# New due times for a delta-rule and two-FFN program, and set fetches queued ahead of the store in front of them

## The chip, the cores and the metric

The program runs on one core of one Trainium2 chip. The metric is the device time of one execution in microseconds (us); for the kernel before, three runs were taken, and one more execution was recorded by the hardware profiler. The engines are TensorE (PE; its weight loads are PEld), VectorE (DVE), ScalarE (ACT), GpSimd (POOL) and SyncE (SP), which here issues most of the DMAs.

## What is computed

The reference runs three parts one after another, in float32. First a delta-rule recurrence over 768 positions for 4 x 8 heads of width 40, then a squared-ReLU FFN (320 to 2048 to 320) on 3072 tokens, then a second FFN that mixes four domains by given probabilities:

```python
for t in range(S):
    y[:, :, t] = np.einsum('bhd,bhde->bhe', rt, state)
    Sa = np.einsum('bhde,bhe->bhd', state, at)
    state_decay = state * wt[:, :, None, :] - np.einsum('bhd,bhe->bhde', Sa, bt)
    state = state_decay + np.einsum('bhd,bhe->bhde', vt, kt)
...
h = x @ w_in
r = np.maximum(h, 0.0)
g = r * r
return (g @ w_out).astype(np.float32)
...
p = domain_probs / (domain_probs.sum(-1, keepdims=True) + 1e-09)
for e in range(E):
    h = np.maximum(x @ w1[e], 0.0)
    out += p[:, e:e + 1] * (h @ w2[e])
```

## The kernel before

**First half.** The 768 positions are cut into 12 chunks of 64 and two batch halves, which gives 24 "steps"; two steps (one chunk) make a "block", so there are 12 blocks. A step multiplies small matrices on PE: `m` (L545, L547), `vm` (L593, L597), `f` (L624), `kbt` (L610), `x` (L637), `merge1` (L679), `merge2` (L691), `tx` (L714), `ys` (L726) and `s` (L754), with copies on ACT and masks, scans and reciprocals on DVE (`vmm` L602, `txm` L718, `P` L488, `rq` and `rs` L508). The triangular inverse inside a chunk is done for a whole block at once on DVE: `m` leaves PE, is copied by ACT and stored to DRAM (`mo`, L563, tile md), loaded back turned (`tl`, L791, tile mu), worked on by 62 dependent DVE operations (`t`, L808 and L811), turned by ACT (`tt`, L818), stored (`to`, L823, tile td) and loaded into the two steps (`ti`, L832, eight DMAs into t and TT). Only then can `merge1` and `merge2` of the two steps run, and behind them `tx`, `x`, `ys` and the new state. A block's result is gathered by twelve DMAs (`tx1`, L919) and split into two float32r parts (`x1h` L930, `x1l` L933); the first FFN then runs 16 "units" on it, each of 8 matmuls `l1` (L317), squaring on ACT (L870 to L875), a difference `gl` on DVE (L878), and 6 matmuls `l2` (L322, L323, L326). In the first 150 us, 48 weight pieces are prepared as well (`w_ld` L345, DVE operations L371 to L378, PE `w_pe` L358 to L360).

**What sets the order.** All of these operations are given to `Schedule`, which replays them on a model of the engines while the program is built and so fixes the order in which each engine's instructions stand; on the chip each engine works through its own list in that order. At every turn the replay takes the engine that can start first and, among its operations that could start within `DELAY` of that, the one with the earliest due time. A due time is the block's or step's base, from `DUE`, less an entry of `LEAD`; an operation of PE in another array tiling than the last counts as due `STAY` later, and up to `COLD` the replay counts PE at half speed. The numbers in these tables are durations in no program: they only choose the order.

**Second half.** The second FFN has 6 pairs of token blocks and 4 weight "sets" for each of 4 domains, so 96 steps. A step is a Strassen-like product of 28 or 32 matmuls (`products` L1225 to L1228, or `plain` L1269 to L1272), whose sums DVE makes (L1233), and 24 matmuls `pz` (L1294 to L1296) of the step before. Its tiles stay in SBUF; 16 sets do not fit, so while a domain runs, the four sets of the next one are prepared one after another (`prepare`): SP loads the raw weights (`set_load`, L1065 and L1066 to L1067, tiles wm and wr), DVE sums them (`set_sum`), ACT rounds them (`set_round2` from wr and `set_round` from wm, L1019), DVE takes the low parts (L1022), and for three of the four SP stores the finished set to DRAM (`set_store`, L1104) because all four are built in the same spare tiles; POOL fetches them later (`set_fetch`, L1108). POOL also fetches each pair's X from DRAM (`x_fetch`, L1197). A class `Beside` deals these jobs out to the steps by a number `due`, by what they depend on, and by `lag`: so many steps must lie between a job and the one that it depends on, if that is on another engine. Before the change a set's load depended on the store of the set in front:

```python
l = job("sp", 0.9, set_load, n, deps=prev, after=after, due=D[0])
w = [job(rnd, 0.36, set_round2, s, i, deps=[l], lag=2, due=D[2], after=s.free) for i in range(2)]
...
if store:
    return [job("sp", 1.8, set_store, s, deps=lo, lag=0, due=D[4])]
return lo + [d]
```

Of the kernel before, what the change touches and what calls it, by code (L numbers as in the profile page):

```python
# [14 lines left out]
B, H, S, D = 4, 8, 768, 40  # L15
# [27 lines left out]
def sub(base, dims):  # L43
# [2 lines left out]

DUE = dict(block=63.76, step=[98.3, -158.9, 2.4, -355.2, -9], invert=[-219.9, -0.6, -157.6], ffn=0.2, w=[-205.6, 1.33])
LEAD = dict(  # L50
    ld_wd=894.9, ld_in=421.6, scan=77.5, m=303, t_load=135.5, t=345.2, t_out=384.9, ld_r=-259.7, ld_xv=-166,
    vm=93.4, f=84.3, kbt=47.4, x=66.9, merge=66.1, tx=131.2, ys=374.4, yq=75.2, x1=185.5,
    split=112.7,
)
DELAY = dict(PE=0.21, ACT=0, DVE=0, POOL=0, SP=0.53)


class Schedule:

    COLD = 54.3  # L60
    STAY = 20.28
    SAME = 0.033

    TILING = dict(vm=1, f=1, tx=1, x=2, ys=2, m=3, merge1=4, merge2=4)
# [10 lines left out]
        m=(.58, .65), vm=(.985, 1.12), kbt=(.41, .6), tx=(.775, .94), f=(.62, .67), merge1=(.62, .69), merge2=(.62, .69),  # L75
        s=(.44, .62), kb=(1.18, 1.25), yq=(.70, .74), scale_a=(1.22, 1.27), yf=(.41, .45), te=(.95, .9), yg=(.16, .2),
# [3 lines left out]
        ld_in=(.43, 2.85, 1.67), ld_r=(.42, .94, 1.45), ld_rf=(.45, .6, 1.65), ld_v=(.45, 1.0, 1.3), ld_wd=(.43, 1.08, 1.35),  # L80
        ld_xv=(1.28, .55, 1.9), mo=(.46, .33, .91), ti=(.46, .28, 1.35), tl=(.58, 1.44, 1.62), to=(.70, 1.05, 1.19),
# [3 lines left out]
        DVE=("P", "t", "x1l", "sq", "w_clamp", "w_shift", "w_sign", "w_pow", "w_mul"),  # L85
        POOL=("scale_a", "kb", "yq", "yf", "y1d", "yg"),
# [103 lines left out]
class Beside:  # L190
# [5 lines left out]
    def job(self, eng, dur, fn, *a, deps=(), lag=1, due=0, after=-99, key=None, via=None):  # L196
        self.n += 1
        key = key or self.n
        engs = (eng,) if isinstance(eng, str) else eng
        self.jobs[key] = (due, self.n, engs, dur, fn, a, deps, lag, after, via)  # L200
        return key
# [66 lines left out]
def tile_delta_rule_moe(  # L268
# [15 lines left out]
    pe, act, dve, pool, sp = nc.tensor, nc.scalar, nc.vector, nc.gpsimd, nc.sync  # L284
# [496 lines left out]
    mdd, x1 = {}, {}  # L781
# [190 lines left out]
    nblk = nsteps // 2  # L972
    PB, F0 = DUE["block"], 80.0
    units = NF1 * (nblk - 1)
    for s in range(nsteps):
        attention(s, F0 + PB / 2 * s + DUE["step"][min(s, len(DUE["step"]) - 1)])
    for k in range(nblk):
# [7 lines left out]
    ffn = []  # L985
# [329 lines left out]
    job = plan.job  # L1315
    NP = NF1 + 2

    done = {}
    for P in range(NPAIR):
        k, e = 2 * P, NPW * P  # L1320
        D = {0: (-50, -15, -13, -12, -10, -7, -8, -4, -2, 0, 1), 1: (-11, -9, -10, -8, -1, 1, 1, 3, 4, 5, 5)}.get(
            P, tuple(e + d for d in (-7, -5, -5, -4, -1, -3, -2, -1, 0, -1, 0)))
# [34 lines left out]
        job("sp", 0.45, x_store, P, 6, 7, deps=b6 + [("st", P, 0)], due=e + 5, key=("st", P, 6))  # L1357

    def prepare(s, D, after, rnd, store, prev, single=False):
        n = s.n  # L1360
        l = job("sp", 0.9, set_load, n, deps=prev, after=after, due=D[0])
        w = [job(rnd, 0.36, set_round2, s, i, deps=[l], lag=2, due=D[2], after=s.free) for i in range(2)]
        lo = [job("dve", 0.41, set_low2, s, i, deps=w[i:i + 1], due=D[4]) for i in range(2)]

        def part(x, y, deps, due, after, lag=1):
            r = [job(rnd, 0.05 + (y - x) / 960, set_round, s, c, x, y, deps=deps, due=due[0], after=after, lag=lag) for c in range(2)]
            q = job("dve", 0.07 + (y - x) / 960, set_rest, s, x, y, deps=r[1:], due=due[1])
            lows = [(max(x, a), min(y, b)) for a, b in ((0, 384), (384, 768), (768, 896)) if max(x, a) < min(y, b)]
            return r + [q] + [job("dve", 0.07 + (b - a) / 960, set_low, s, a, b, deps=r[:1], due=due[1]) for a, b in lows]

        d4 = D[2], D[4]
        if not single:
            m = [job('dve', 0.72, set_sum, n, *z, deps=[l], lag=2 if after >= 0 else 3, due=D[1]) for z in SUMS]
            lo += part(0, 384, m, d4, s.free) + part(384, 896, m, d4, s.free)
            d = job("sp", 0, set_done, s, deps=lo, lag=0, due=D[4], key=("set", n))
        else:
            lo += part(0, 512, [l], d4, s.free, lag=2)
            d = job("sp", 0, set_done, s, deps=lo, lag=0, due=D[4], key=("set", n))
        if store:
            return [job("sp", 1.8, set_store, s, deps=lo, lag=0, due=D[4])]  # L1380
        return lo + [d]

    homes, spare = list(range(NPW)), NPW
    prev = []
    for n in range(NPW):
        s = Set(n, homes[n], 3 * homes[n] + 4 - NP)
        D = ((-14, -18, -10, -9, -7), (-9, -10, -4, -2, -2), (-8, -5, 2, 2, 1), (-7, -1, 1, 1, 2))[n]
        prepare(s, D, -NP - 1, ("dve", "act"), False, [], True)
    for e in range(NE - 1):
        for i in range(NPW):  # L1390
            n = NPW * (e + 1) + NPW - 1 - i
            b = PER * e + (4 if e == 0 else 0) + 5 * i
            prev = prepare(Set(n, spare, b), tuple(b + d for d in ((0, 8, 8, 8, 8) if e else (-2, 0, 5, -7, 0))), b, ("act",), i < NPW - 1, prev)
# [3 lines left out]
    for G in range(NPAIR, NE * NPAIR):  # L1397
        e, i = divmod(G, NPAIR)
# [4 lines left out]
    i = -NP  # L1403
# [131 lines left out]
```

## Time and profile before

| | |
|---|---|
| median of 3 runs | 1474.74 us (1464.42 to 1477.5) |
| profiled execution | 1474.95 us |
| its span, first to last instruction | 1473.2 us |
| PE / DVE / ACT / POOL busy | 1381.4 / 1082.5 / 785.1 / 207.8 us |
| mean granted clock of PE | 0.971 |

The span falls into a start of some 216 us, in which the weights are prepared and the first blocks run, a steady part up to 752 us with one block after another, and the second FFN. "Granted clock" is the share of TensorE's full 2.4 GHz that was given; it has two levels here, 1.0 and 0.5 (1.2 GHz), so a mean between them tells how long the lower one held. In the chain of waits, "DMA x<-y" is a transfer from its issue to its landing, and SPq is SP issuing. In a timeline the bracket behind a row is the engine's idle time before it and what ended that.

### The profile page before, as it was taken

What the parts mean: (1) busy time and instruction counts of PE and PEld (TensorE: products, weight loads), DVE (VectorE), ACT (ScalarE), POOL (GpSimd) and SP (SyncE); (2) the same over time, 40 slices, a digit from 0 to 9 for tenths busy, and PEclk for the clock granted to TensorE, in tenths of its full rate; (3) what the DMA queues carried; (4) which work ended last, traced back from release to release, by engine and by line L of the source; (5) the groups of instructions that cost most, each with busy time, mean ns of one, the idle gap of its engine ahead of it and who ended that gap; (6) DMA issues with size and microseconds to landing.
All of it is one profiled execution on the core that took longest, in us unless ns stands there. A gap on an engine that the chain in (4) does not pass through costs nothing.

```text
span 1473.2 us, 39713 instructions
## 1 busy us (share of the span) xinstructions
PE 1381.4 (94%) x16072; PEld 1312.5 (89%) x16072; DVE 1082.5 (73%) x2664; ACT 785.1 (53%) x1933; POOL 207.8 (14%) x327
## 2 busy tenths in 40 slices
PE   4698999989999999999989999999999999999998
PEld 3476888888888888898989999999999999999998
DVE  7889868778788687686648556667667776866665
ACT  5486767777777676686667445533223333322221
POOL 4120311312312312221000000100001000010000
PEclk9989989999999899998999999999999999999999
DMA  8465342442543433433142344565435244344220
GB/s 248 112 196 173 91 119 63 135 124 68 136 127 74 124 110 102 119 81 80 27 150 92 117 182 172 196 224 229 154 141 200 80 190 183 125 131 168 112 93 37
DMA packets 154679, 194.61 MB, mean 132 GB/s; under 512 B 97536, under 2 KB 118272, under 8 KB 152192
## 3 DMA queue, kind: packets, MB, share of 16 engines
q1 hardware_dynamic: 147584, 140.76, 31.2%
q0 software_dynamic: 6912, 51.32, 9.5%
q8 instruction: 127, 2.08, 0.6%
q14 instruction: 56, 0.46, 0.1%
HBM read 138.35 MB, written 48.96 MB: 127 GB/s over the span
## 4 chain that ended last, share of the span: by engine, by line
PE 60%; DVE 12%; DMA 12%; ACT 7%; SPq 4%; issue 3%; POOL 1%; DVEq 0%; ACTq 0%
PE pz L1295 7%; PE pz L1296 7%; PE pz L1294 7%; PE Q L1225 4%; PE h L317 4%; PE Q L1227 4%; PE Q L1228 4%; PE Q L1226 4%; DVE t L811 3%; DVE tmp L808 3%; DMA td<-mu 2%; DMA wr<-wf 2%; DVE gl L878 2%; PE px L637 2%; DMA TT<-td 2%
## 5 line engine op out<-in xcount | busy, mean ns | idle before, releaser
L1233 DVE TENSOR_TENSOR C<-C,Q 128x256 f32<-128x256 f32 (+1 forms) x432 | 181.9, 463 | 134.9 <-PE Q L1228 112.9
L1294 PE MATMUL pz<-w,z 128*128 128x320 f32 x768 | 238.0, 310 | 0.0
L1295 PE MATMUL pz<-w,z 128*128 128x320 f32 x768 | 237.6, 309 | 0.0
L1296 PE MATMUL pz<-w,z 128*128 128x320 f32 x768 | 237.5, 309 | 0.0
L317 PE MATMUL h<-xh,w 128*128 128x256 f32 x960 | 199.1, 290 | 0.0
L1239 ACT ACTIVATE z<-C 128x512 fp32r<-128x512 f32 x144 | 91.2, 633 | 166.7 <-DVE C L1233 164.6
L317 PE MATMUL h<-xl,w 128*128 128x256 f32 x576 | 164.3, 286 | 0.6 <-DVE xl L933 0.6
L317 PEld LDWEIGHTS h<-xh,w 128*128 128x128 f32 x960 | 158.0, 193 | 2.3
L878 DVE TENSOR_TENSOR gl<-r,gh 128x256 fp32r<-128x256 f32 x192 | 89.7, 467 | 79.4 <-ACT r L875 61.4
L1225 PE MATMUL Q<-X,w 128*128 128x256 f32 x504 | 141.5, 281 | 4.2 <-ACT C L1244 4.2
L1294 PEld LDWEIGHTS pz<-w,z 128*128 128x128 f32 x768 | 144.6, 188 | 0.0
L1295 PEld LDWEIGHTS pz<-w,z 128*128 128x128 f32 x768 | 144.5, 188 | 0.0
L1296 PEld LDWEIGHTS pz<-w,z 128*128 128x128 f32 x768 | 144.2, 188 | 0.0
L1226 PE MATMUL Q<-X,w 128*128 128x256 f32 x504 | 141.4, 281 | 0.0
L1228 PE MATMUL Q<-X,w 128*128 128x256 f32 x504 | 141.4, 280 | 0.0
L322 PE MATMUL py<-w,gh 128*128 128x320 f32 x384 | 127.1, 338 | 4.8 <-ACT gh L873 4.8
L1244 ACT COPY C<-Q 128x256 f32<-128x256 f32 x72 | 26.8, 372 | 178.0 <-PE Q L1228 178.0
L1227 PE MATMUL Q<-X,w 128*128 128x256 f32 x432 | 121.2, 281 | 0.0
L323 PE MATMUL py<-w,gh 128*128 128x320 f32 x384 | 117.9, 315 | 0.0
L317 PEld LDWEIGHTS h<-xl,w 128*128 128x128 f32 x576 | 111.6, 194 | 0.8 <-DVE xl L933 0.8
L870 ACT ACTIVATE r<-h 128x256 f32<-128x256 f32 x192 | 73.0, 380 | 62.6 <-PE h L317 54.9
L326 PE MATMUL py<-w,gl 128*128 128x320 f32 x384 | 94.0, 327 | 11.9 <-DVE gl L878 11.5
(145 smaller groups left out, 3494.5 us busy)
## 6 DMA issues: line engine op xcount, KB each, us to landing
X<-xsd POOLq DMA_DIRECT2D x12, 2688.0 KB, 9.9
in<-kba SPq DMA_DIRECT2D x24, 768.0 KB
wsd<-w SPq DMA_DIRECT2D x27, 640.0 KB
w<-wsd POOLq DMA_DIRECT2D x27, 640.0 KB, 6.9
xsd<-X SPq DMA_DIRECT2D x6, 2304.0 KB
raw<-wm SPq DMA_DIRECT2D x32, 234.0 KB
wm<-wf SPq DMA_DIRECT2D x13, 512.0 KB
wd<-w SPq DMA_DIRECT2D x24, 264.0 KB
```

The source lines that it names most:

```text
L317: pe.matmul(ps, a, b, start=n == 0, stop=n == len(mm) - 1)
L322: pe.matmul(pys[tt], gh[:, sl], t[:, 256:576], start=first, stop=False)
L323: pe.matmul(pys[tt], gh[:, sl], t[:, 960:1280], start=False, stop=False)
L878: dve.tensor_tensor(g["gl"], g["r"], g["gh"].bitcast(F32), ALU.subtract)
L1225: pe.matmul(o, hi, x[:, 0], start=True, stop=False)
L1226: pe.matmul(o, hi, x[:, 2], start=False, stop=False)
L1227: pe.matmul(o, v.low(i), x[:, 0], start=False, stop=False)
L1228: pe.matmul(o, c, x[:, 1], start=False, stop=True)
L1233: plus = lambda o, x, y: dve.tensor_tensor(o, x, y, ALU.add)
L1294: pe.matmul(py2[0][t], gh[:, sl], hi, start=j == f == 0, stop=False)
L1295: pe.matmul(py2[0][t], gh[:, sl], lo, start=False, stop=False)
L1296: pe.matmul(py2[0][t], gl[:, sl], hi, start=False, stop=j == NPW - 1 and f == 1)
```

## The change

Two things. First, the tables `DUE`, `LEAD`, `DELAY`, `COLD` and `STAY` get new numbers; no operation of the first half is added or taken away, only the order in the engines' lists changes. Second, in `prepare` a set's load no longer depends on the store of the set in front but on the operations that the store depends on, so that it can stand ahead of the store; the rounds, which write the tiles that the store reads, now depend on the store instead (`kept`), and the two `set_round2` come three steps behind the load instead of two.

```diff
-DUE = dict(block=63.76, step=[98.3, -158.9, 2.4, -355.2, -9], invert=[-219.9, -0.6, -157.6], ffn=0.2, w=[-205.6, 1.33])
+DUE = dict(block=61.4, step=[38.8, -203.7, -45, -290.9, -0.9], invert=[-168.3, 104.5, -49.1], ffn=3.7, w=[-113.4, 1.12])
...
     def prepare(s, D, after, rnd, store, prev, single=False):
+        prev, kept = prev
         n = s.n
-        l = job("sp", 0.9, set_load, n, deps=prev, after=after, due=D[0])
-        w = [job(rnd, 0.36, set_round2, s, i, deps=[l], lag=2, due=D[2], after=s.free) for i in range(2)]
+        l = job("sp", 0.9, set_load, n, deps=prev, lag=0, after=after, due=D[0])
+        w = [job(rnd, 0.36, set_round2, s, i, deps=[l] + kept, lag=2 if single else 3, due=D[2], after=s.free) for i in range(2)]
...
-            r = [job(rnd, 0.05 + (y - x) / 960, set_round, s, c, x, y, deps=deps, due=due[0], after=after, lag=lag) for c in range(2)]
+            r = [job(rnd, 0.05 + (y - x) / 960, set_round, s, c, x, y, deps=deps + kept, due=due[0], after=after, lag=lag) for c in range(2)]
...
         if store:
-            return [job("sp", 1.8, set_store, s, deps=lo, lag=0, due=D[4])]
-        return lo + [d]
+            kept = [job("sp", 1.8, set_store, s, deps=lo, lag=0, due=D[4])]
+        return lo + [d], kept
```

Three places show how the lists move. The first is SP in the start, from the loads ahead of the second block's md back to mu: md and mu are the tiles of the inverse's round trip, xr<-y the gathering of the first block's result, raw the weight pieces, xv, r, v, rf, in and wd a step's inputs. Before:

```order
L563 DMA md_505<-mb_1298 32x8x32 x4
L345 DMA raw_0_1355<-wm 128x472
L465 DMA xv_1398<-vn 64x8x40
L466 DMA xv_1398<-vn 64x8x40
L791 DMA mu_1415<-md_505 64x1024
L345 DMA raw_1_1422<-wm 128x468
L791 DMA mu_1415<-md_505 64x1024
L450 DMA r_1455<-rv 128x512
...
L919 DMA xr_1477<-y_1302 40x256 x3
```

The same place after:

```order
L919 DMA xr_1406<-y_1309 24x256
L446 DMA wd_1521<-w 128x528
L919 DMA xr_1406<-y_1309 40x256
L439 DMA in_1535<-kba 128x1536
L345 DMA raw_0_1557<-wm 128x472
L345 DMA raw_1_1561<-wm 128x468
L345 DMA raw_2_1567<-wm 128x468
L345 DMA raw_0_1573<-wm 128x472
L450 DMA r_1575<-rv 128x512
L461 DMA v_1579<-rv 128x512
L791 DMA mu_1582<-md_505 64x1024
L345 DMA raw_1_1597<-wm 128x468
```

The second block's loads of mu stood right behind the stores of md; now all twelve gathering DMAs, four weight loads and four input loads stand between.

The second place is PE in a steady block, around the first merge (py<-TT is `merge1`, pt<-y `merge2`, pm is `m` of the odd step of the next block, ptx is `tx`; h, py<-w,gh and py<-w,gl are the first FFN). Before:

```order
L326 MATMUL py_1_7204<-w_674,gl_4_7410 128x320
L545 MATMUL pm_7422<-in_7254 32x64 x2
...
L547 MATMUL pm_7443<-in_7254 32x64 x2
L679 MATMUL py_7469<-TT_89,m_5830 32x32 x16
L317 MATMUL h_6_7491<-xh_7022,w_802 128x256
...
L691 MATMUL pt_7507<-y_7500,t_7390 32x32 x16
L679 MATMUL py_7532<-TT_90,m_6412 32x32 x16
L322 MATMUL py_0_7203<-w_741,gh_5_7397 128x320
...
L714 MATMUL ptx_0_7561<-x_7039,TT_89 64x104 x2
```

The same place after:

```order
L610 MATMUL pk_7391<-cs,in_6189 128x128 x4
L545 MATMUL pm_7405<-in_7238 32x64 x2
...
L547 MATMUL pm_7429<-in_7238 32x64 x2
L322 MATMUL py_0_7203<-w_674,gh_4_7329 128x320
...
L326 MATMUL py_1_7204<-w_674,gl_4_7403 128x320
L679 MATMUL py_7468<-TT_89,m_5831 32x32 x16
...
L691 MATMUL pt_7505<-y_7497,t_7377 32x32 x16
L322 MATMUL py_0_7203<-w_741,gh_5_7396 128x320
...
L714 MATMUL ptx_1_7539<-x_7043,TT_89 64x104 x2
L679 MATMUL py_7562<-TT_90,m_6398 32x32 x16
```

An `l2` of the FFN (L322 to L326) now lies between the pm and the first merge, and the second step's `merge1` moved from in front of the next `l2` to behind the first step's `tx`. Further on (not shown) the first step's `s` moved from behind the second step's `tx` to ahead of it, with one `l1` between.

The third place is SP in the second half, where one set's store and the next set's load meet (wsd is the store, wm and wr the load). Before:

```order
L1104 DMA wsd<-w_1172 128x1280
L1104 DMA wsd<-w_1361 128x1280
L1104 DMA wsd<-w_1548 128x1280
L1104 DMA wsd<-z_13527 128x128
L1066 DMA wm_15942<-wf 128x2x512
L1067 DMA wr_15943<-wf 128x640
```

After:

```order
L1066 DMA wm_16006<-wf 128x2x512
L1067 DMA wr_16007<-wf 128x640
L1104 DMA wsd<-w_1172 128x1280
L1104 DMA wsd<-w_1463 128x1280
L1104 DMA wsd<-w_1706 128x1280
L1104 DMA wsd<-z_13527 128x128
```

The load now stands ahead of the store. It is so at six of the nine places where a load and a store meet; at the three of the first domain the load stays behind.

## Rows read from the trace of the kernel before

**Rows 1.** Busy time by stretch, steady part: us, busy (instructions), PEclk, DMA share, GB/s.

```profile
216.00:752.00 536.00, 503.00 (x8192) 463.18 (x8191) 409.62 (x1082) 381.24 (x1010) 117.44 (x182) 0.96 0.36 96
```

**Rows 2.** Chain of waits through one steady block: start us, us, what.

```profile
430.03 3.43 DMA td<-mu
...
445.74 4.66 DMA mu<-md
```

**Rows 3.** Chain of waits: the turn by ACT that ends a block's inverse, four of eleven.

```profile
199.98 1.07 ACT mu L818
...
428.20 1.08 ACT mu L818
...
483.14 1.07 ACT mu L818
...
713.17 1.09 ACT mu L818
```

**Rows 4.** Busy time by stretch: PE, PEld, DVE, ACT, POOL, then PEclk, DMA share, GB/s.

```profile
488.40:493.00 4.60, 2.16 (x70) 1.55 (x69) 3.47 (x6) 3.00 (x10) 0.77 (x1) 1.00 0.66 191
493.00:504.00 11.00, 10.81 (x178) 9.77 (x180) 5.64 (x9) 3.92 (x10) 2.59 (x2) 0.53 0.60 164
...
450.40:483.10 32.70, 30.93 (x395) 28.95 (x392) 30.40 (x93) 25.00 (x68) 4.23 (x7) 1.00 0.27 71
107.30:139.80 32.50, 26.68 (x207) 21.07 (x206) 31.37 (x128) 24.56 (x73) 1.66 (x3) 0.90 0.63 204
173.70:199.90 26.20, 25.31 (x203) 23.80 (x204) 23.37 (x80) 19.91 (x54) 0.00 (x0) 1.00 0.25 72
```

**Rows 5.** Timeline of PE around the first merge of two blocks, and `tx` of the second step.

```profile
437.09 0.84 PE L679 MATMUL py<-TT,m 32*32 32x32 f32 x32 [0.80 <-DMA TT<-td]
...
447.28 0.94 PE L714 MATMUL ptx<-x,TT 64*64 64x104 f32 x32
...
493.06 1.46 PE L679 MATMUL py<-TT,m 32*32 32x32 f32 x32 [1.97 <-DMA TT<-td]
...
507.16 0.94 PE L714 MATMUL ptx<-x,TT 64*64 64x104 f32 x32
```

**Rows 6.** Groups by line: what, count | busy us, mean ns | idle before, releasers.

```profile
L322 PE MATMUL py<-w,gh 128*128 128x320 f32 x384 | 127.1, 338 | 4.8 <-ACT gh L873 4.8
...
L602 DVE TENSOR_TENSOR xv<-pv,cs 64x512 f32<-64x512 f32 x96 | 64.2, 686 | 2.4 <-PE pv L597 0.8
L718 DVE TENSOR_TENSOR xv<-ptx,cs 64x416 f32<-64x416 f32 x96 | 55.1, 587 | 32.0 <-PE ptx L714 30.3
...
L508 DVE RECIPROCAL q<-P 128x128 f32<-128x128 f32 x48 | 44.5, 934 | 0.0
...
L754 PE MATMUL pst<-cs,ST 128*128 128x128 f32 x88 | 14.0, 282 | 0.0
```

**Rows 7.** Timeline of SP in the start: start us, us, line, issue.

```profile
102.06 0.50 SPq L791 DMA_DIRECT2D mu<-md  x1
...
105.47 7.66 SPq L919 DMA_DIRECT2D xr<-y  x10
...
115.37 1.82 SPq L345 DMA_DIRECT2D raw<-wm  x4
```

**Rows 8.** Timeline of DVE in the start: the second inverse's first operation.

```profile
107.34 0.20 DVE L808 TENSOR_TENSOR tmp<-mu,t 128x31 f32<-128x31 f32 x1 [0.50 <-DMA mu<-md]
```

**Rows 9.** Chain of waits in the second half: the load of a set's second part.

```profile
1047.81 13.79 DMA wr<-wf
```

**Rows 10.** Timelines of ACT and PE where that load is waited for, and the second such place.

```profile
1061.69 0.82 ACT L1019 CAST w<-wr 128x320 fp32r<-128x320 f32 x2 [5.89 <-DMA wr<-wf]
...
1062.83 0.43 PE L1225 MATMUL Q<-X,w 128*128 128x256 f32 x1 [2.80 <-ACT C L1244]
...
1229.28 0.38 PE L1225 MATMUL Q<-X,w 128*128 128x256 f32 x1 [1.37 <-ACT C L1244]
```

**Rows 11.** Busy time right behind the first of these waits, columns as in rows 4.

```profile
1062.80:1066.30 3.50, 3.47 (x16) 3.48 (x17) 2.85 (x7) 0.83 (x2) 0.00 (x0) 0.53 0.00 0
```

More of the change, by code (lines that the diff above doesn't have):

```diff
@@ L44, in sub @@
     return AP(base.tensor, base.offset, [list(base.ap[0])] + dims)
-DUE = dict(block=63.76, step=[98.3, -158.9, 2.4, -355.2, -9], invert=[-219.9, -0.6, -157.6], ffn=0.2, w=[-205.6, 1.33])
+DUE = dict(block=61.4, step=[38.8, -203.7, -45, -290.9, -0.9], invert=[-168.3, 104.5, -49.1], ffn=3.7, w=[-113.4, 1.12])
 LEAD = dict(
-    ld_wd=894.9, ld_in=421.6, scan=77.5, m=303, t_load=135.5, t=345.2, t_out=384.9, ld_r=-259.7, ld_xv=-166,
-    vm=93.4, f=84.3, kbt=47.4, x=66.9, merge=66.1, tx=131.2, ys=374.4, yq=75.2, x1=185.5,
-    split=112.7,
+    ld_wd=780.7, ld_in=268.5, scan=105.8, m=150.1, t_load=194.1, t=282.2, t_out=539.7, ld_r=-151.6, ld_xv=46.4,
+    vm=91.4, f=70.9, kbt=51.1, x=69.3, merge=70, tx=194.8, ys=289.6, yq=40, x1=539.5,
+    split=111.2,
 )
-DELAY = dict(PE=0.21, ACT=0, DVE=0, POOL=0, SP=0.53)
+DELAY = dict(PE=0.3, ACT=0, DVE=0, POOL=0, SP=1.5)
 class Schedule:
-    COLD = 54.3
-    STAY = 20.28
+    COLD = 57.5
+    STAY = 18.91
     SAME = 0.033
@@ L1379, in prepare @@
         if store:
-            return [job("sp", 1.8, set_store, s, deps=lo, lag=0, due=D[4])]
-        return lo + [d]
+            kept = [job("sp", 1.8, set_store, s, deps=lo, lag=0, due=D[4])]
+        return lo + [d], kept
     homes, spare = list(range(NPW)), NPW
-    prev = []
+    prev = [], []
     for n in range(NPW):
@@ L1387, in tile_delta_rule_moe @@
         D = ((-14, -18, -10, -9, -7), (-9, -10, -4, -2, -2), (-8, -5, 2, 2, 1), (-7, -1, 1, 1, 2))[n]
-        prepare(s, D, -NP - 1, ("dve", "act"), False, [], True)
+        prepare(s, D, -NP - 1, ("dve", "act"), False, ([], []), True)
     for e in range(NE - 1):
```

## Prediction

> **What bounds the kernel now.** I began with the busy time by stretch. In the steady part [rows 1] PE is busy 503.0 of 536 us (its weight loads 463.2, beside the matmuls), DVE 409.6, ACT 381.2. The mean granted clock is 0.96, and as its levels are 1.0 and 0.5, the lower one holds for (1 - 0.96) / 0.5 x 536 = some 43 us. Next come the chain of waits through one block [rows 2] and the turns by ACT that end each inverse [rows 3]. The chain is a loop with no PE in its longest pieces: the turned inverse is stored (430.03, 3.43 us to land), loaded into the steps, the next block's m is stored and loaded back (445.74, 4.66), and then DVE works on the inverse from 450.40 to 483.14, where ACT's turn begins. That window is 32.7 us long and DVE is busy 30.40 of it [rows 4], so it is a chain of dependent DVE work with other DVE work in the holes. From the turn at 199.98 to that at 713.17 there are nine blocks, so a block takes 513.19 / 9 = 57.0 us; the block from 428.20 to 483.14 takes 54.9.
>
> What makes the difference of 2.1 us? The timeline of PE shows it [rows 5]. In the good block PE waits 0.80 us for TT ahead of the first merge at 437.09, and the second step's `tx` starts at 447.28, 10.2 us later. In another PE waits 1.97 us at the same place, and `tx` comes 14.1 us later (493.06 to 507.16). Just before, PE was busy 2.16 of 4.6 us, and from 493 to 504 its clock was granted at 0.53, the lower level, while PE was busy 10.81 of 11 us [rows 4]. As the DVE window cannot close before the `txm` that follows that `tx`, a block loses 14.1 - 10.2 = 3.9 us by such a fall. Over nine blocks 9 x 2.1 = 18.7 us are lost, which is 4.8 falls; 43 us of lower clock are about as many stretches of some 10 us.
>
> In the second half PE is nearly full. Its waits for a set are two: 2.80 us at 1062.83 and 1.37 at 1229.28, both for a copy by ACT [rows 10]. ACT stood 5.89 us ahead of the first, in the rounding that needs wr; that load took 13.79 us [rows 9], queued behind the store of the set in front. After the wait PE ran 3.50 us at 0.53 [rows 11].
>
> **The start.** SP works through its list, and the second block's load of mu was issued at 102.06 [rows 7]. Ahead of it now stand twelve gathering DMAs, of which ten took 7.66 us, so 12 x 0.766 = 9.2; four weight loads, 1.82 for four; and four input loads, at the 0.50 of the load beside them 2.0. That gives 102.06 + 13.0 = about 115. The first operation of the inverse came 107.34 - 102.06 = 5.3 us behind it [rows 8], so it now comes at 120.4; DVE has masks in front of it that wait for FFN units of PE, for which I add 2.6 (bounds 0 and 6). So it starts at 123, 16 us later. Its window was 32.5 us with DVE busy 31.37 and 128 instructions [rows 4]. Reciprocals and weight operations that lay in it now lie in front; I take 29 us, the middle between the third block's 26.2 and 32.5. The inverse then ends at 152 instead of 139.8, 12 late. From there to the next window, 139.8 to 173.7, 33.9 us passed, more than the 57.0 - 32.7 = 24.3 of a steady block; so PE's list held the loop up by 9.6 us. Two of the `m` and two FFN units now stand further forward in that list, so I let the 9.6 be given back whole: 12 - 9.6 = 2.4 late. The third window (26.2 us, DVE busy 23.37) gains one reciprocal (0.934) and four `vmm` (4 x 0.686), 3.7 in all [rows 6], of which 2.8 fill its idle time at best; I count them nearly in full, as they stand between dependent operations: +2.6. The start costs 2.4 + 2.6 = **+5**. At best the masks cost nothing (2.6 less), the second window takes 26.2 (2.8 less) and the third is not longer (2.6 less), which gives 3 back; if the first delay is never made good, the start costs 16.
>
> **The steady blocks.** In a steady block DVE's list loses one reciprocal (0.934) from the inverse's window, which now stands in front of it, and takes one more `txm` (0.587) into it [rows 6]: 0.35 less in each of nine blocks, **-3**. The first step's `s` now stands in front of the second `tx`; its PE instructions are cheap (88 take 14.0 us [rows 6], 0.16 each, four to a step: 0.64), and DVE's first operation of the inverse stands one `txm` (0.587) earlier, so the two cancel. As for the falls of the clock, PE's idle time ahead of the first merge is cut in two: an `l2` now stands between the `m` and that merge, and the merge of the second step no longer stands directly in front of FFN work but behind the first `tx`. This cannot be read from a trace that does not have it. Its bounds are nothing and all 4.8 falls, and below nothing too, 4.2 blocks more that could fall. I take two falls fewer, near half of what there is, because only in some blocks is PE's wait as short as the 0.80 us that kept 1.0: 2 x 3.9 = **-7.8**.
>
> **The end of the first half.** Behind the last `merge1` six `l2`, those of one unit, more are left; at 127.1 / 384 = 0.33 each [rows 6] that is 2.0 if all of it lies bare, and nothing if it fills waits of the last state work. I take the middle, **+1**.
>
> **The second half.** At six of nine meetings the load goes first. The bytes are the same (a store is 3 x 655 + 66 KB, a load 524 + 328 KB), so the store now ends about where the load ended, and the rounding, which now waits for it, could only change what it waits for. What helps is the third step between load and rounding: 24 steps lie between the two PE waits, so a step is (1229.28 - 1062.83) / 24 = 6.9 us, more than ACT's 5.89. Both waits go, 2.80 + 1.37 = 4.2 us, and with the first the 3.50 us at 0.53, which at 1.0 would be 1.9: 1.6. Together **-5.8**. The spare is 6.9 - 5.9 = 1.0 us before ACT waits again and 6.9 - 2.8 = 4.1 before PE does. The cost of a rounding that comes late is covered by the set being needed only in the next domain.
>
> The page "DMA: Bandwidth & Descriptors" of the Trainium skill says, in its section on queues and rings, that within one queue each engine starts descriptors in order. By that a load put ahead lands sooner and the store later by as much, and the change of order alone would be worth nothing here; 13.79 us for the load behind the store agrees [rows 9]. The gain then hangs on the third step alone, as above.
>
> **Sum.** 5 - 3 - 7.8 + 1 - 5.8 = -10.6, and 1474.95 - 10.6 = 1464.3. The profiled execution took 1474.95 us for a span of 1473.2, 0.2 above the median of the three runs, so the same sum stands for that.
>
> **Rivals.** (a) The falls of the clock all go. For it: an uninterrupted PE keeps 1.0, as from 450 to 483 [rows 4], and what preceded the fall was 2.16 us of work in 4.6. Against it: TT still has to land, and PE must have something to do till then. Then -18.7 stands for -7.8: 1453.5. In the Trainium skill, "TensorE: Matmul & The Clock Gate" (Part 1) calls the throttled state the default that activity releases; by it the broken-up wait would favour this rival. The rows' 1.00 and 0.53 agree with two levels; none has the new order.
>
> (b) The new tables trade one thing for another and the first half nets nothing: the start's cost eats what the blocks give. Then only -5.8 is left, 1469.2. For it: most of the loop is DMA and dependent DVE work, which no order shortens. Against it: 2.1 us a block that the better blocks do not spend.
>
> (c) Slower. The second inverse's 13 us of SP queue are never recovered, since each block's inverse follows the one before; the late results leave PE without work at the merges, and the falls stay: 16 - 3 + 1 - 5.8 = +8.2, 1483.2. It decides from where the start's cost passes 3 + 5.8 - 1 = 7.8 with no fall saved. For it: rows 2 and 3 show a loop with no slack. Against it: the 9.6 us that PE's list held in the start.
>
> (d) In the second half the wait only takes another name, the store's: 0 instead of -5.8, 1470.2. For it: equal bytes, a spare of 1.0 on ACT. Against: 4.1 on PE.
>
> **Chances.** My forecast 0.42, own range 1457 to 1472; (a) 0.22, (b) 0.18, (c) 0.13, (d) 0.05. The range goes from below (a) to (c), 1448 to 1482; less than 2 in 10 lies beyond. About 1% (14.7 us) is what a measurement of this kernel can tell, as the three runs lie 0.9% apart. Faster than 1460.2: nearly all of (a) and a fifth of the forecast, 0.30. Slower than 1489.5: the far part of (c), 0.08. The rest, 0.62, is the same.
>
> **What would show it.** Right: the second load of mu near 115 and the first operation of its inverse near 123; ACT's second and third turns near 152 and 205 instead of 139.8 and 199.98; blocks of 55 to 56 us behind them; a clock above 0.96 between 216 and 752; no PE wait at L1225 of over 1 us and wr's load landing in under 13.79 us. Wrong: a third turn before 200 or after 212, a clock of 0.96 or below, blocks of 57 us, a product in the second half that waits for ACT with a store as its cause. Were the falls still there with `merge1` behind `tx`, the step on the clock would be wrong; were the turns late throughout by 16, that on the start.

## The result, and the profile after

The changed kernel took 1459.51 us in the median of twelve runs (1450.58 to 1466.66), the kernel before 1473.59 beside it (1464.42 to 1477.88). The ratio is 0.9903, with a 95% interval of 0.9882 to 0.9924: 14.1 us or 1.0% faster. The forecast was 10.6 us less. The profiled execution of the changed kernel took 1465.54 us, 6 above its median, with a span of 1463.8.

The busy time by stretch of the changed kernel answers to [rows 1, 4]: us, then PE, PEld, DVE, ACT and POOL busy, the granted clock, the DMA share and GB/s. The second and third lines are the windows of the second and third inverse, the fourth that of a steady block, the last two the time just before and just behind a first merge.

```profile
216.00:752.00 536.00, 508.45 (x8248) 470.29 (x8246) 404.54 (x1083) 381.70 (x1021) 114.48 (x182) 0.96 0.37 99
123.50:149.40 25.90, 19.47 (x86) 12.89 (x87) 25.87 (x126) 14.57 (x46) 0.00 (x0) 1.00 0.44 135
174.20:203.30 29.10, 28.39 (x351) 27.25 (x343) 27.36 (x87) 24.57 (x71) 2.59 (x4) 1.00 0.34 100
450.40:482.80 32.40, 31.53 (x411) 29.86 (x410) 30.09 (x93) 25.51 (x70) 3.81 (x7) 1.00 0.29 85
487.50:492.60 5.10, 2.83 (x80) 2.20 (x80) 4.89 (x9) 3.33 (x11) 1.03 (x1) 1.00 0.43 126
492.90:500.00 7.10, 7.10 (x113) 6.17 (x108) 1.74 (x5) 2.69 (x7) 1.18 (x1) 0.52 0.68 210
```

The steady clock is 0.96 as before: in this one execution the falls to the lower clock are still there (the last two lines show one). PE is busy 508.45 for 503.00 of the same 536 us, but a second trace of the kernel before has 506.16 there, so one execution can account for most of that. The next lines are the turns by ACT that end the inverses, from the timeline of ACT; they answer to [rows 3].

```profile
149.31 1.11 ACT L818 COPY mu<-t 128x512 f32<-128x512 f32 x1 [0.32 <-DVE t L811]
203.24 1.07 ACT L818 COPY mu<-t 128x512 f32<-128x512 f32 x1 [0.68 <-DVE t L811]
428.22 1.08 ACT L818 COPY mu<-t 128x512 f32<-128x512 f32 x1 [0.65 <-DVE t L811]
482.70 1.07 ACT L818 COPY mu<-t 128x512 f32<-128x512 f32 x1 [0.67 <-DVE t L811]
708.75 1.08 ACT L818 COPY mu<-t 128x512 f32<-128x512 f32 x1 [0.43 <-DVE t L811]
```

The third turn is 3.3 us later than before (203.24 for 199.98), the last 4.4 earlier (708.75 for 713.17): nine blocks took 505.5 us, 56.2 each instead of 57.0. The start, in SP's and DVE's timelines, answers to [rows 7, 8]:

```profile
98.00 8.46 SPq L919 DMA_DIRECT2D xr<-y  x11
...
107.07 1.79 SPq L919 DMA_DIRECT2D xr<-y  x1
...
109.49 1.80 SPq L345 DMA_DIRECT2D raw<-wm  x4
...
112.29 0.52 SPq L791 DMA_DIRECT2D mu<-md  x1
...
113.81 0.50 SPq L791 DMA_DIRECT2D mu<-md  x1
```

```profile
122.88 0.69 DVE L602 TENSOR_TENSOR xv<-pv,cs 64x512 f32<-64x512 f32 x1
123.60 0.20 DVE L808 TENSOR_TENSOR tmp<-mu,t 128x31 f32<-128x31 f32 x1
```

The gathering DMAs and the weights stand in front of mu, and the masks (L602) in front of the first operation of the inverse. PE's timeline around the merges of the two blocks of [rows 5] reads now:

```profile
437.22 0.79 PE L679 MATMUL py<-TT,m 32*32 32x32 f32 x32 [0.94 <-DMA TT<-td]
...
448.69 0.94 PE L714 MATMUL ptx<-x,TT 64*64 64x104 f32 x32
...
492.53 0.73 PE L679 MATMUL py<-TT,m 32*32 32x32 f32 x30 [1.60 <-DMA TT<-td]
...
505.89 0.94 PE L714 MATMUL ptx<-x,TT 64*64 64x104 f32 x32
```

In the second half (where the title's fetches are SP's loads, `set_load`, and not POOL's `set_fetch`), the groups of PE and ACT show what became of [rows 9, 10]. The last number is the idle time in front of the group:

```profile
L1225 PE MATMUL Q<-X,w 128*128 128x256 f32 x504 | 141.0, 280 | 0.0
...
L1019 ACT CAST w<-wr 128x320 fp32r<-128x320 f32 x25 | 10.1, 451 | 0.0
```

Both waits are gone; a small new one, 0.5 us in all, stands in the group of L1227:

```profile
L1227 PE MATMUL Q<-X,w 128*128 128x256 f32 x432 | 121.2, 281 | 0.5 <-DVE w L1022 0.5
```

In the kernel before, the first two groups read:

```profile
L1225 PE MATMUL Q<-X,w 128*128 128x256 f32 x504 | 141.5, 281 | 4.2 <-ACT C L1244 4.2
...
L1019 ACT CAST w<-wr 128x320 fp32r<-128x320 f32 x25 | 10.2, 453 | 10.3 <-DMA wr<-wf 10.3
```

So one pair of traces shows the second half's gain, the start's loss and some gain in the blocks, but no fewer falls of the clock. Whether falls become fewer, and what they cost, had to come from more runs.

### The profile page after: what moved, and what is told of

It reads as the page before. It is cut to its first block, busy times and chain, and to the rows that moved or that the text cites. A ratio compares the mean times of both kernels' runs of the same rounds, so it can differ in the third digit from the quotient of the medians.

```text
span 1463.8 us, 39707 instructions
## 1 busy us (share of the span) xinstructions
PE 1379.9 (94%) x16072; PEld 1310.9 (90%) x16072; DVE 1076.2 (74%) x2664; ACT 781.2 (53%) x1933; POOL 200.8 (14%) x327
## 4 chain that ended last, share of the span: by engine, by line
PE 65%; DMA 10%; ACT 9%; DVE 9%; SPq 4%; issue 3%; POOL 0%; ACTq 0%; DVEq 0%; POOLq 0%
PE pz L1295 8%; PE pz L1296 8%; PE pz L1294 8%; PE h L317 5%; PE Q L1227 4%; PE Q L1228 4%; PE Q L1226 4%; PE Q L1225 4%; DMA td<-mu 2%; DMA TT<-td 2%; PE px L637 2%; PE pys L726 2%; DVE t L811 2%; DVE tmp L808 2%; SPq L919 2%
## 5 line engine op out<-in xcount | busy, mean ns | idle before, releaser
L1225 PE MATMUL Q<-X,w 128*128 128x256 f32 x504 | 141.0, 280 | 0.0
L322 PE MATMUL py<-w,gh 128*128 128x320 f32 x384 | 129.3, 344 | 2.6 <-ACT gh L873 1.9
L1227 PE MATMUL Q<-X,w 128*128 128x256 f32 x432 | 121.2, 281 | 0.5 <-DVE w L1022 0.5
L326 PE MATMUL py<-w,gl 128*128 128x320 f32 x384 | 91.9, 321 | 8.6 <-DVE gl L878 8.3
```

Of the source, the lines that this page charges most:

```text
L322: pe.matmul(pys[tt], gh[:, sl], t[:, 256:576], start=first, stop=False)
L326: pe.matmul(pys[tt], gl[:, sl], t[:, 256:576], start=False, stop=last)
L1225: pe.matmul(o, hi, x[:, 0], start=True, stop=False)
L1227: pe.matmul(o, v.low(i), x[:, 0], start=False, stop=False)
```

## Experiments

The table has each run with its ratio to the kernel before on the same chip; the clock is the mean granted clock of the whole program, averaged over the runs of that kernel. The runs were made on several chips. The kernel before took 1473.6 to 1474.0 us in the median on most of them, but 1470.15 on the one of `filler 6`, `mu first` and the two lag runs, so kernels are compared by the ratio and not by the medians.

| kernel | median us | ratio (95% interval) | clock |
|---|---|---|---|
| before, again | 1472.31 | 0.9992 (0.9963 to 1.0022) | 0.975 |
| changed | 1459.51 | 0.9903 (0.9882 to 0.9924) | 0.981 |
| prepare only | 1467.90 | 0.9953 (0.9925 to 0.9981) | 0.974 |
| tables only | 1468.19 | 0.9961 (0.9933 to 0.9989) | 0.979 |
| l2 back | 1464.19 | 0.9936 (0.9907 to 0.9965) | 0.976 |
| filler 12 | 1458.59 | 0.9903 (0.9865 to 0.9941) | 0.987 |
| filler 6 | 1455.53 | 0.9892 (0.9868 to 0.9917) | 0.988 |
| old tables, filler | 1456.54 | 0.9886 (0.9849 to 0.9923) | 0.987 |
| filler 6, early | 1449.68 | 0.9847 (0.9803 to 0.9891) | 0.991 |
| filler elsewhere | 1458.58 | 0.9904 (0.9872 to 0.9935) | 0.982 |
| mu first | 1519.54 | 1.0332 (1.0302 to 1.0362) | 0.970 |
| lag 2 (one run) | 1453.49 | none | 0.987 |
| lag 3 only (one run) | 1476.29 | none | 0.969 |

**The kernel before, again.**

> The kernel before, unchanged, to have the granted clock of each of its runs. Theory (the changed kernel gained in the first half by fewer stretches at the lower clock): its runs lie near 1473.6 us with a mean clock near 0.971, against 0.973 to 0.989 in the twelve runs of the changed kernel, and the slower of its runs are those with the lower clock. Rival (the clock of the profiled pair, 0.971 against 0.975, is all there is, and the rest is order): the clock of these runs spreads as widely and as high as that of the changed kernel, and the time does not follow it.

The times follow the clock: of the twelve runs the quickest, 1461.15, had 0.984, and the slowest, 1480.86, had 0.969. A straight line through the twelve gives 1.1 us for each 0.001 of clock, through the twelve of the changed kernel 0.96. The mean clock is 0.975 here and 0.981 there; 29 further runs of the kernel before had 0.972. The two ranges overlap (0.969 to 0.984 and 0.973 to 0.989), so the rival is right that a single pair shows nothing, and the theory is right on the average, where the changed kernel spends less time at the lower clock.

**The two parts by themselves.** The first run is the changed kernel with all the old tables and the new `prepare`, the second has the new tables and the old `prepare` (both diffs are against the changed kernel and shown in part):

```diff
-DUE = dict(block=61.4, step=[38.8, -203.7, -45, -290.9, -0.9], invert=[-168.3, 104.5, -49.1], ffn=3.7, w=[-113.4, 1.12])
+DUE = dict(block=63.76, step=[98.3, -158.9, 2.4, -355.2, -9], invert=[-219.9, -0.6, -157.6], ffn=0.2, w=[-205.6, 1.33])
...
```

```diff
-        l = job("sp", 0.9, set_load, n, deps=prev, lag=0, after=after, due=D[0])
+        l = job("sp", 0.9, set_load, n, deps=prev, after=after, due=D[0])
...
-            kept = [job("sp", 1.8, set_store, s, deps=lo, lag=0, due=D[4])]
-        return lo + [d], kept
+            return [job("sp", 1.8, set_store, s, deps=lo, lag=0, due=D[4])]
+        return lo + [d]
```

> Only the second half of the change: the old tables, with the new prepare. Theory: both waits of PE for ACT in the second half go and nothing else moves, so 5 to 6 us less than before, a ratio near 0.9963, and the stretch behind 752 us takes 717 us as in the changed kernel instead of 722. Rival one (the wait only takes the store's name): ratio 1.000. Rival two (the second half's gain came from where the first half ends): ratio above 0.998.

> Only the first half of the change: the new tables, with the old prepare. Theory: the rest of the gain, 14.1 - 5.5 = 8 to 9 us less than before, a ratio near 0.994, with the two waits of 2.8 and 1.4 us at L1225 back. Rival (the tables net nothing and the gain sits in the second half): ratio 0.999 to 1.001.

They gave 0.9953 and 0.9961, that is 6.9 and 5.7 us, 12.6 together against 14.1 for both at once: the parts add up within their intervals, and each is clear of 1. With `prepare` alone PE waits nowhere at L1225; with the tables alone it waits again:

```profile
L1225 PE MATMUL Q<-X,w 128*128 128x256 f32 x504 | 141.3, 280 | 3.4 <-ACT C L1244 3.4
```

The second half can also be read by itself, with far less noise than the totals have: from the start of its first product matmul to the end of the span. That matmul, first in the kernel before, then with `prepare` alone:

```profile
788.68 0.28 PE L1269 MATMUL Q<-X,w 128*128 128x256 f32 x1
```

```profile
787.78 0.28 PE L1269 MATMUL Q<-X,w 128*128 128x256 f32 x1
```

With spans of 1473.2 and 1466.7 us that is 684.5 and 678.9. A second trace of the kernel before has 685.3, the one with the tables alone 682.2, and every trace with the whole new `prepare` 678.9 or 679.0. So the new `prepare` takes 5.5 to 6.4 us from the second half.

The tables' 5.7 us go with a clock of 0.979 for 0.975.

**Order of load and store, or the third step.** The first run takes the third step out of the changed kernel, the second puts it alone into the kernel before:

```diff
-        w = [job(rnd, 0.36, set_round2, s, i, deps=[l] + kept, lag=2 if single else 3, due=D[2], after=s.free) for i in range(2)]
+        w = [job(rnd, 0.36, set_round2, s, i, deps=[l] + kept, lag=2, due=D[2], after=s.free) for i in range(2)]
```

```diff
-        w = [job(rnd, 0.36, set_round2, s, i, deps=[l], lag=2, due=D[2], after=s.free) for i in range(2)]
+        w = [job(rnd, 0.36, set_round2, s, i, deps=[l], lag=2 if single else 3, due=D[2], after=s.free) for i in range(2)]
```

> The changed kernel, but the two set_round2 two steps behind the load again; the load stays ahead of the store. Theory (the third step alone brings the gain, as the bytes are the same and the rounding now waits for the store): a wait of PE at L1225 for ACT comes back, one or two of 1 to 3 us, with a store as what ACT waits for, and the stretch behind 752 us grows by 2 to 5 us. Rival (the order alone brings it, the load landing early): no wait of PE over 0.5 us between 800 and 1460 us, and the second half takes 717 us as in the changed kernel.

> The kernel before with the two set_round2 of the later sets three steps behind the load instead of two; the load still waits for the store. Theory (the third step alone brings the gain): both waits of 2.8 and 1.4 us at L1225 are gone and the second half takes 717 us instead of 722. Rival (the order is needed): one or both waits stay, the first at 1 us or more.

With the order alone, PE's group at L1225 and the one long wait of ACT that makes it are:

```profile
L1225 PE MATMUL Q<-X,w 128*128 128x256 f32 x504 | 141.1, 280 | 0.8 <-ACT C L1244 0.8
```

```profile
1206.70 0.82 ACT L1019 CAST w<-wr 128x320 fp32r<-128x320 f32 x2 [3.95 <-DMA wsd<-w]
```

ACT does wait for the store now, as expected, but all such waits of ACT come to 4.3 us in two places. With the same tables and the old `prepare` they were 5.00 and 4.57, at 1047.75 and 1212.81: the later one is nearly whole (3.95), the earlier one gone. PE loses 0.8 us instead of 3.4. With the third step alone, in the kernel before, it loses 1.4 instead of 4.2, and for DVE instead of ACT:

```profile
L1225 PE MATMUL Q<-X,w 128*128 128x256 f32 x504 | 141.3, 280 | 1.4 <-DVE C L1233 1.4
```

Either of the two takes away most of the wait at L1225 and neither all of it; both together leave 0.0. The second half, counted as above, takes 679.4 us with the order alone (682.2 without), 680.9 with the third step alone (684.5 and 685.3 without) and 678.9 with both. That the order alone is worth nothing fell. Why the store lands early enough in that run was not settled: the jobs also came to stand in other steps than before, and so otherwise to the X fetches. (The totals of these two runs say little, since their clocks were 0.987 and 0.969 in the one execution taken.)

**Fillers in front of the merge.** Twelve matmuls whose product is overwritten stand in front of the first merge of a block, in the place where PE waits for TT:

```diff
                 py = d["py"] = psa.tile([128, 8, 32], F32, tag="at", name=f"py{s}")
+                if hb == 0 and k >= 3:
+                    xf = x1[max(x1)][0]
+                    for _ in range(12):
+                        pe.matmul(py.rearrange("p a x -> p (a x)"), wt[0][:, 0:128], xf[:, 0], start=True, stop=True)
```

> The changed kernel, with twelve extra matmuls of 128 columns by 256 put in front of the first merge of each block from the fourth on; their product is overwritten and changes no output. They fill some 1.5 us of the 1.2 to 1.7 us in which PE stands there for TT. Theory (the lower clock comes from PE standing between the small matmuls ahead of that merge): the falls behind the merges from 271 to 673 us become fewer, the clock between 216 and 752 us rises from 0.96 to 0.98 or more, and the time falls by 3 to 10 us against the changed kernel, to 1450 to 1456. Rival one (the falls have another cause): the clock stays at 0.96 and the time within 2 us of the changed kernel. Rival two (PE has less slack there than it seems, and the fillers hold the merge up): up to 9 x 1.5 = 13 us slower than the changed kernel, 1473.

The steady stretch and the place in front of a merge (the fillers are the first line, the merge the second):

```profile
216.00:752.00 536.00, 513.24 (x8465) 474.84 (x8465) 412.50 (x1102) 388.19 (x1036) 116.05 (x186) 1.00 0.39 105
```

```profile
438.41 1.59 PE L679 MATMUL py<-xh,w 128*128 128x256 f32 x12
439.94 0.69 PE L683 MATMUL py<-TT,m 32*32 32x32 f32 x32
...
443.40 0.94 PE L718 MATMUL ptx<-x,TT 64*64 64x104 f32 x32
```

The clock of the steady part is 1.00 for 0.96 in these two executions; the mean of all runs, 0.987 for 0.981, carries the reading, and it is what the theory on the cause foresaw. The time gains nothing clear, 1458.59 for 1459.51 with the same ratio: by the line of 0.96 us for each 0.001, a clock of 0.987 for 0.981 is worth some 6 us, and 5 of them are given back. The merge starts right behind the last filler, without a wait, so it can be the fillers that hold it up. Six of them, from the third block on:

> As the run with twelve fillers, but six, and from the third block on instead of the fourth. With twelve no fall was left behind a merge, PE waited nowhere for TT, and an undisturbed block took some 0.5 us more than without. Theory (twelve were longer than the wait and held the merge up): six, 0.75 us, keep most falls away without holding anything up; the clock stays at 0.985 or more and the time comes to 1451 to 1456. Rival (six leave a wait of 0.5 to 1 us, and the falls are back): a clock of 0.981 and 1457 to 1460, as the changed kernel.

1455.53 us at 0.988. The clock is what the theory says, and four blocks in a row without a fall took 53.7 to 54.2 us where the same four took 54.1 to 55.0 with twelve (one trace each), which fits that twelve held the merge up. The time doesn't settle it: the kernel before is quicker on this chip too, and by the ratio (0.9892 for 0.9903) the gain on the changed kernel is 1.6 us, inside the intervals. The control puts the same six, from the first block to the eleventh, in the middle of the inverse's window, in front of an `l1`:

```diff
+        if f == 10 and k < NBLK - 1:
+            for _ in range(6):
+                pe.matmul(ps, wt[0][:, 0:128], x1[k][0][:, 0], start=True, stop=True)
         ffn1(ps, wt[f], *x1[k][:2])
```

> A control: the changed kernel with the same six extra matmuls in each block from the first to the eleventh, but in front of the first FFN's eleventh l1, in the middle of the inverse's window, where PE does not stand for TT. Theory (fillers help because they stand in front of the wait): the falls behind the merges stay, the clock at 0.979 to 0.983, and the time within 3 us of the changed kernel's mean of 1459.3 or a little above. Rival (any more work of this kind holds the clock up): clock 0.988 or more and 1450 to 1456, as with the fillers in front of the merge.

1458.58 us at 0.982: as the changed kernel without any fillers. It is the mean clock that sets the place in front of the merge apart (0.982 for 0.988, eight and six runs). The times don't (0.9904 for 0.9892), and neither does one trace: the control's steady part has 0.99, and three of its nine blocks a fall, as many as with the six in front of the merge.

```profile
216.00:752.00 536.00, 508.72 (x8373) 471.00 (x8373) 410.07 (x1099) 386.58 (x1033) 115.77 (x186) 0.99 0.39 103
```

Fillers in front of the merge do two things at once, though: they fill the wait, and they put full-size matmuls between small ones. Which of the two keeps the clock up was not tested.

**What in the new tables keeps the clock.** One pair of traces showed no fewer falls. There are more traces without fillers: four of the old first half (`before`, `before again`, `prepare only`, `lag 3 only`) and three of the new (`changed`, `tables only`, `lag 2`). Between ACT's third and eleventh turns lie nine blocks, and a block counts as having a fall where its granted clock is under 1.00: 26 of 36 with the old order, 12 of 27 with the new. The steady part of the kernel before [rows 1] and of the changed one have 0.96; in `tables only` and `lag 2` it reads:

```profile
216.00:752.00 536.00, 506.50 (x8355) 467.19 (x8355) 411.02 (x1102) 387.63 (x1035) 115.99 (x186) 0.98 0.39 105
```

```profile
216.00:752.00 536.00, 505.49 (x8319) 465.53 (x8314) 410.78 (x1101) 388.08 (x1035) 116.07 (x186) 0.99 0.40 106
```

Leaving out the last of the nine blocks, which is shorter in nearly every trace, the old order's blocks took 54.7 to 55.8 us without a fall and 57.3 to 59.6 with one. (Two of the three new traces are quick executions, so the count flatters the new order; the mean clocks say the same with a smaller difference.)

If the tables bring nothing but fewer falls, fillers make up for them. And if it is the `l2` between m and the first merge that does it, putting that back undoes them:

```diff
+        for k in range(3, 11):
+            l, m = ("l2", k - 1, 4), ("m", 2 * k + 3, 0)
+            i, j = order.index(m), order.index(l)
...
+                order.insert(i, order.pop(j))
         for n in order:
             ops[n][1]()
```

> The old tables with the new prepare, and six fillers in front of the first merge of each block from the third on. Theory (what the new tables bring is nothing but fewer falls): the falls behind the merges go here too, the clock rises from 0.974 to 0.985 or more and the time from 1466.5 (the mean of the runs with prepare alone) to 1452 to 1457, level with the new tables and the same fillers. Rival (the new order shortens the loop itself): the clock rises, but the time stays 4 us or more above that of the new tables with six fillers, 1459 or more.

> The changed kernel, but on PE the six matmuls l2 that stand between the odd step's m and the first merge stand ahead of that m again, as before the change, in the fourth to the eleventh block; nothing else moves. Theory (that l2 breaks up the stretch of small matmuls, so that the clock falls less often): the clock goes back from 0.981 to 0.975 or less and the time up by 4 to 8 us, to 1463 to 1467. Rival one (the other moves, such as the second step's merge1 behind the tx, keep the clock): clock 0.980 to 0.982 and 1457 to 1461. Rival two (the l2 ahead of m delays m, the load of mu and so the loop): each block 0.5 to 1 us longer at the same clock, 4 to 8 us in all.

The old tables with fillers come to a ratio of 0.9886 at 0.987, the new ones with the same fillers to 0.9892 at 0.988; the difference is far inside the intervals. With the `l2` back the clock goes to 0.976 and the time to 1464.19. That is the expected size, 4.7 us of the 8.4 that lie between `prepare` alone and the changed kernel; but the intervals of this run and of the changed kernel overlap, so it points to the `l2` and doesn't prove it. PE stands as long ahead of the merges as in the changed kernel. First the changed kernel, then the one with `l2` back (whose lines are 6 further on), the idle time again last:

```profile
L679 PE MATMUL py<-TT,m 32*32 32x32 f32 x768 | 19.6, 198 | 15.0 <-DMA TT<-td 15.0
```

```profile
L685 PE MATMUL py<-TT,m 32*32 32x32 f32 x768 | 21.8, 207 | 15.0 <-DMA TT<-td 14.0 <-ACT mb L562 0.5
```

These two executions also had nearly the same clock, 0.975 and 0.974, so the pair doesn't tell whether the sum of the waits decides or what stands on either side of them.

**The start.** One due time is changed, that of the second block's inverse:

```diff
-DUE = dict(block=61.4, step=[38.8, -203.7, -45, -290.9, -0.9], invert=[-168.3, 104.5, -49.1], ffn=3.7, w=[-113.4, 1.12])
+DUE = dict(block=61.4, step=[38.8, -203.7, -45, -290.9, -0.9], invert=[-168.3, -157.6, -49.1], ffn=3.7, w=[-113.4, 1.12])
```

> The changed kernel with the due time of the second block's inverse 262 us earlier (-157.6 for 104.5), so that its loads of mu stand ahead of the gathering DMAs again and its DVE operations 32 places further forward; the rest follows by itself. Theory (the late second inverse costs the start the 3 to 5 us that the third turn of ACT is late): the second turn near 140 instead of 150.4, the third near 200 instead of 204.3, and 2 to 5 us less in all. Rival one (the list of PE holds the loop up there anyway): the second turn is 10 us earlier and the third within 1 us of 204, the time the same. Rival two: what DVE had pulled forward now falls into the third window, which is longer, and the kernel is up to 5 us slower.

None of the three: 1519.54 us. The second turn is as early as expected, but the third is late, and every block after that is slow:

```profile
139.44 1.07 ACT L818 COPY mu<-t 128x512 f32<-128x512 f32 x1
...
213.76 1.10 ACT L818 COPY mu<-t 128x512 f32<-128x512 f32 x1 [0.17 <-DVE t L811]
```

A steady window of this kernel, with the masks (L602) and the `txm` (L718) in DVE's groups for that window:

```profile
417.60:466.50 48.90, 42.35 (x681) 37.91 (x676) 45.31 (x109) 32.05 (x85) 12.83 (x18) 0.90 0.35 104
```

```profile
L602 DVE TENSOR_TENSOR xv<-pv,cs 64x512 f32<-64x512 f32 x8 | 5.5, 686 | 0.2
...
L718 DVE TENSOR_TENSOR xv<-ptx,cs 64x416 f32<-64x416 f32 x8 | 4.7, 589 | 0.5 <-PE ptx L714 0.3
```

The same two groups in the changed kernel's window from 450.40 to 482.80:

```profile
L602 DVE TENSOR_TENSOR xv<-pv,cs 64x512 f32<-64x512 f32 x4 | 2.7, 686 | 0.1
...
L718 DVE TENSOR_TENSOR xv<-ptx,cs 64x416 f32<-64x416 f32 x3 | 1.8, 590 | 0.1
```

The window takes 48.9 us for 32.4, with DVE busy 45.31 for 30.09. All eight masks and all eight `txm` of a block now stand inside it for four and three, and eight reciprocals for five. The replay came into another steady pattern, from one due time in the start, and stayed in it. What the late second inverse by itself costs was therefore not measured; rival two named the mechanism, but for the third window alone and with a tenth of the size.

**A kernel that beats both.** In four of the traces with the new tables a stretch of some 10 us at the lower clock stood at 160 us, behind the merge of the second block. Six fillers from that block on (`k >= 1`):

> As the run with six fillers, from the second block on. Theory (the stretch of 10.2 us at the lower clock behind the merge at 160 us, seen in three runs with the new tables, is of the same kind): it goes, the third turn of ACT comes near 204 instead of 208, and the time falls by 2 to 5 us to 1451 to 1454. Rival (the start is held by other work): within 1 us of 1455.5.

1449.68 us, 0.9847 (0.9803 to 0.9891, four runs), at a clock of 0.991. The steady part is at 1.00, and the turns show the start without its fall and nine blocks of 54.2 us:

```profile
216.00:752.00 536.00, 510.00 (x8388) 472.51 (x8387) 413.44 (x1107) 391.88 (x1044) 115.84 (x186) 1.00 0.40 107
```

```profile
203.32 1.08 ACT L822 COPY mu<-t 128x512 f32<-128x512 f32 x1 [0.66 <-DVE t L815]
...
691.39 1.08 ACT L822 COPY mu<-t 128x512 f32<-128x512 f32 x1 [0.43 <-DVE t L815]
```

(691.39 - 203.32) / 9 = 54.2. It is the best of all, 10 us below the changed kernel in the medians and 8 by the ratio; with four runs the two intervals just overlap.

## Why the prediction was right, and where it was not

**The start** came nearly as worked out. The load of mu was issued at 112.29 for a forecast of 115, the first operation of its inverse at 123.60 for 123. Two errors of about 3 us cancel there, which is luck: the operation came 11.3 us behind the load, for 7.9 in the forecast. The second inverse's window was 25.9 us, below the 29 that was taken, the second turn at 149.31 for 152, the third at 203.24 for 205: +3.3 for +5. The step that let PE's list give 9.6 us back held: the second turn was 9.5 us late, the third window began 0.5 late (174.2 for 173.7) and took 29.1 us for 26.2, +2.9 for +2.6.

**The steady window** gained what was forecast, a little less in sum. From DVE's first operation to ACT's turn, six of the nine windows took 32.7 us (one of the six 33.0) in all four traces of the old order and 32.2 to 32.3 in all three of the new: some 0.5 less for 0.35. But the first of the nine became 0.9 to 1.9 us longer, which the forecast doesn't have, so about 2 us are gained for 3.

**The falls.** By the prediction's own signs the profiled execution says wrong: the clock is 0.96, where "0.96 or below" was a sign against it, and with `merge1` behind `tx` the falls are still there. The further traces and the mean clocks say that this one execution misled, and that the step holds on the average: 12 of 27 blocks with a fall for 26 of 36, that is 4.0 in nine for 6.5, and a mean clock of 0.979 to 0.981 for 0.975. The forecast counted 4.8 falls at 3.9 us each and took two fewer; the old order's traces show more falls, at some 2.9 us each (the mean of its blocks with a fall less that of those without). That the number of falls to go was right is partly luck, as the prediction says itself that it could not read it from the trace. That the clock matters is shown by the fillers: with the old tables they take the ratio from 0.9953 to 0.9886 and the clock from 0.974 to 0.987. That the `l2` between `m` and the merge is what does it in the new order is likely, not shown.

**The end** was +1. From the last turn to the first product of the second half it took 74.6 to 75.8 us with the old order and 75.5 to 76.1 with the new, which allows the +1 and doesn't show it.

**The second half** had the right size by a partly wrong step. 5.8 us were forecast; read by itself it gained 5.5 to 6.4, and both waits at L1225 went. The step that failed is the one that called the change of order worth nothing because the bytes are equal: alone it brought PE's wait from 3.4 to 0.8 us, and the third step alone brought it from 4.2 to 1.4. At the later place the step held (ACT waited 3.95 us for 4.57), at the earlier it didn't (nothing for 5.00). That the wait takes the store's name was right, as the trace with two steps shows. The rule of the Trainium skill, "DMA: Bandwidth & Descriptors" (Queues, rings and completion order), that descriptors of one queue start in order, is contradicted by no row here; what was drawn from it, that the change of order is worth nothing, is contradicted by the 0.8 us. When wr's load landed, one of the signs, the changed kernel's trace doesn't show, as nothing waited for it.

**The sum.** -10.6 was forecast and -14.1 measured, with an interval of -17.4 to -11.2 by the ratio. The direction and the parts held, the size was somewhat small. As the second half gained 5.5 to 6.4 us, some 8 are left for the first half, for 4.8 in the forecast; what is short is there. The start, the windows and the end nearly cancel (+3, -2, +1), so it is the falls that gave more than 7.8, some 10 by difference, with an uncertainty of 3 us from the interval.

**The rivals.** (a) The falls going altogether was not what the tables did. Fillers did it in the nine blocks of the best kernel's trace, and that kernel came to 1449.68 where (a) said 1453.5. (b) A first half that nets nothing is out: 11.2 us at least were gained in all, and the second half gained 6.4 at most. (c) The late start that is never made good is out by the third turn. Its price of 16 was also too high by the prediction's own terms, since an inverse that ends 12 late and a third window 2.6 longer come to 14.6. (d) The wait that only takes another name is out by the group at L1225 and by the 678.9 us.

## What to carry to other kernels

Where PE is the busiest engine but stands at one place in a loop, look at the granted clock behind that place, and try a little work that can be thrown away right in front of the wait: here six matmuls a block on the old tables (0.9886) were worth at least as much as refitted due times (0.9903). Before one pair of traces is read for such a thing, look at how time and clock go together over a dozen runs. And where a greedy replay sets the order, a single due time in the start can put every later block into another pattern, so compare the window of a steady block, not only the start.

## What was not expected of the hardware

Twelve runs of one and the same kernel spread over 1.3% (1461.15 to 1480.86 us), and TensorE's clock goes with it: 0.969 to 0.984, with 1.1 us for each 0.001, a line that takes up nine tenths of the variance (three quarters in the twelve of the changed kernel). The falls come mostly at the same place of a block, behind the first merge, but not in the same blocks of each execution, although the program is the same: of the nine blocks behind the third turn, the first, third and sixth to ninth had one in one trace of the kernel before, and the first, second, fourth, fifth, seventh and eighth in another. Nor is a trace in which falls are rare a sign of a better program: the new first half had 0.96, 0.98 and 0.99 in three executions.
